# Waiting for the output store at the end of a decode kernel: the wait moves from SyncE to GpSimd

## The chip, the cores and the metric

One core of one Trainium2 chip. The metric is the device time of one execution in microseconds (us). A run can fall into a slower state with a lower granted clock; no run whose state is on record did (granted clocks of 0.766 to 0.771 of full speed), so all of them may be compared. Times inside a trace are counted from the first instruction of the program.

The engines are TensorE (PE in the profile), VectorE (DVE), ScalarE (ACT), GpSimd (POOL) and SyncE (SP). A q behind the name (SPq, POOLq) means the engine's sequencer, which runs its program, waits and issues transfers (DMA). A semaphore is a counter: one side raises it, and another waits until it has reached a value. A barrier is a place that no engine passes before all have reached it.

## The reference

One decoding step: a layer norm of one token, grouped attention over a cache of 65,536 keys and values in eight groups, an output projection, a small feed-forward branch, and the sum.

```python
x = A_x                                   # (1, 1, 512)
xn = _layernorm(x)
# _A_ref: q = xn @ wq, 32 heads on 8 cached K/V heads, softmax over 65536 keys, @ wo
# _B_ref: gelu(xn @ w1 + b1) @ w2 + b2
return x + _A_ref(xn, A_k_cache, A_v_cache, A_wq, A_wo) + _B_ref(xn, B_w1, B_b1, B_w2, B_b2)
```

The K and V caches are 134 MB each in bfloat16 (8 x 65,536 x 128 x 2 bytes). The output is 512 numbers, 1 KB.

## The kernel before

A small recording layer collects every operation with what it reads and writes, and works out the semaphore waits. The engines' programs are then emitted, most of them inside a block. A barrier of the program's own stands at the end of the block; behind it follow the last matmuls, the last cast, the store and the wait for it.

```python
# ... (norm, projections, the loop over K and V, the last matmuls into pR)
sch.op(DVE, lambda: dve.tensor_copy(out=fin_bf[0:NR, :], in_=pR[0:NR, 0:128]),     # L823
       reads=[f"pss{R}"], writes=["fin"])
ev_out = sch.dma(
    SP,
    lambda: sp.dma_start(out=out[0, 0].rearrange("(kt p) -> kt p", p=128),         # L827
                         in_=fin_bf[0:NR:32, :]),
    sem_out, reads=["fin"], writes=["out_dram"],
)
# ...
with nc.Block() as block:                                                          # L842
    # ... each engine's program up to here
    # ...
for e, obj in ((PE, pe), (DVE, dve), (SP, sp)):
    _emit(obj, e.ops[rest[e]:])
sp.wait_ge(ev_out.sem, ev_out.val)                                                 # L866
```

The store's semaphore is number 119; the program waits until it holds 16, which I call full. GpSimd and ScalarE have nothing to do behind the block. GpSimd's last work in the whole kernel is a small memset that passes on the arrival of the last V chunk.

## Time and profile before

| what | before |
|---|---|
| median of the first 3 runs (lowest, highest) | 656.82 us (656.76, 657.03) |
| span of the profiled run, first to last instruction | 655.5 us |
| device time of the same run | 656.81 us |
| read from HBM | 280.50 MB, 428 GB/s |
| last cast / store issued / semaphore full / wait over | 653.79 / 654.46 / 655.46 / 655.49 us |

The page of the kernel before says what bounds it. The DMA row gives the busy share of the DMA engines in 40 slices, in tenths:

```profile
span 655.5 us, 27968 instructions
...
DMA  9999999999999999999999999999999999999997
...
HBM read 280.50 MB, written 0.00 MB: 428 GB/s over the span
## 4 chain that ended last, share of the span: by engine, by line
DMA 63%; PE 34%; issue 2%; DVE 0%; SPq 0%
```

The DMA engines are busy for 90% or more of every slice but the last. Nothing at the end of the kernel can change that; the change can only move the last few microseconds. The chain of waits, in order of time, shows those (start, duration, what; the last pieces, kernel before):

```profile
635.59 17.13 DMA kv<-in_A_wo_dram
652.72 0.14 issue
652.85 0.62 PE pss L805 x16
653.48 0.02 issue
653.50 0.29 DVE fin_bf L823
```

This chain ends with the last instruction that an engine executes, the cast at 653.79 us. It does not hold the store and the wait, which are work of a sequencer. The timeline shows the issue of the store (start, duration, engine, line, what; kernel before):

```profile
653.82 0.64 SPq L827 DMA_DIRECT2D out_dram<-fin_bf  x1
```

And the list of SyncE's own waits shows the wait for it (engine and line, whom it waited for, us in total, times, longest; kernel before):

```profile
SPq L827 <- DVE fin_bf L823: 3.4, 1, 3.4
SPq L866 <- DMA out_dram<-fin_bf: 1.0, 1, 1.0
```

So the span ends with SyncE's wait, at 655.49 us. But the run took 656.81 us, and no view prints what lies in the 1.32 us behind the span. The trace has it all the same: it records every update of every semaphore, those that the program doesn't own too. These are the updates of semaphore 2 near the end, read from these records (us from the span's start; kernel before):

```
first pass :  653.641 653.675 653.714 653.934 | 655.619 655.663 655.701 655.735 655.782
(234 other semaphores, one update each, 655.749 to 656.345)
second pass:  656.569 656.604 656.642 656.685 656.709 656.808 656.846 656.880 656.927
```

I call the updates of a pass moves 1 to 9. The Trainium skill, "Runtime: NRT & Kernel Launch", section "Semaphores 0–2 are reserved", says that semaphore 2 is the runtime's sync barrier. Its section "The ~15µs preamble/postamble breakdown" puts a barrier, a clearing of the semaphores and another barrier behind every kernel, and gives the way through the five engines, for the barrier in front of the kernel, as about 355 ns, 8 hops of 44 ns. This trace agrees in the sum: in the second pass, moves 1 to 9 took 358 ns. The single hops were unequal: 35, 38, 43, 24, 99, 38, 34 and 47 ns. That the single updates between the passes are the clearing is read from their place there and from that section. In nine of the ten profiles of this study the device time is within 0.02 us of move 6 of the second pass (in one, E5, it is 0.135 us later, and why stays open). So I measure the tail from the end of the last wait for the store to that move: 656.808 - 655.493 = 1.315 us before.

### The profile page before, as it was taken

What the parts mean: (1) busy time and instruction counts of PE and PEld (TensorE: products, weight loads), DVE (VectorE), ACT (ScalarE), POOL (GpSimd) and SP (SyncE); (2) the same over time, 40 slices, a digit from 0 to 9 for tenths busy, and PEclk for the clock granted to TensorE, in tenths of its full rate; (3) what the DMA queues carried; (4) which work ended last, traced back from release to release, by engine and by line L of the source; (5) the groups of instructions that cost most, each with busy time, mean ns of one, the idle gap of its engine ahead of it and who ended that gap; (6) DMA issues with size and microseconds to landing.
All of it is one profiled execution on the core that took longest, in us unless ns stands there. A gap on an engine that the chain in (4) does not pass through costs nothing.

```text
span 655.5 us, 27968 instructions
## 1 busy us (share of the span) xinstructions
PE 536.8 (82%) x12682; PEld 509.6 (78%) x12682; DVE 275.8 (42%) x574; ACT 245.0 (37%) x454; POOL 2.9 (0%) x27
## 2 busy tenths in 40 slices
PE   2478699989789697878969788896978879797897
PEld 0277598979788696878959687895978879697886
DVE  3244072625436171453516245261534516154353
ACT  0134162634425162352506235160443516145251
POOL 0000000000000000000000000000000000000000
PEclk9788596967869596786959679595886959578695
DMA  9999999999999999999999999999999999999997
GB/s 386 445 431 422 431 430 432 446 422 450 416 448 420 428 460 404 436 428 454 430 420 440 426 442 422 426 460 408 444 426 450 430 418 436 428 460 404 432 432 305
DMA packets 8774, 280.65 MB, mean 428 GB/s; under 512 B 1082, under 2 KB 1596, under 8 KB 1724
## 3 DMA queue, kind: packets, MB, share of 16 engines
q1 hardware_dynamic: 8616, 280.50, 99.4%
q8 instruction: 8, 0.13, 0.1%
q10 hardware_dynamic: 148, 0.01, 0.0%
q14 instruction: 2, 0.02, 0.0%
HBM read 280.50 MB, written 0.00 MB: 428 GB/s over the span
## 4 chain that ended last, share of the span: by engine, by line
DMA 63%; PE 34%; issue 2%; DVE 0%; SPq 0%
DMA kv<-in_A_k_cache_dram 61%; PE pst L590 27%; PE pss L610 4%; DMA kv<-in_A_wo_dram 3%; PE pO L681 2%; PE pA L637 0%; PE pA L648 0%; DVE pmax L618 0%; PE pA L697 0%; PE pss L805 0%; DVE gmax L639 0%; DVE diag L641 0%; SPq L470 0%; SPq L467 0%; DVE fin_bf L823 0%
## 5 line engine op out<-in xcount | busy, mean ns | idle before, releaser
L600 ACT ACTIVATE kt_ring<-pst 128x1024 bf16<-128x1024 bf16 x192 | 195.6, 1027 | 310.6 <-PE pst L590 309.2
L590 PE MATMUL pst<-ident_bf,kv 128*128 128x128 bf16 x4096 | 281.8, 235 | 34.5 <-DMA kv<-in_A_k_cache_dram 34.4
L590 PEld LDWEIGHTS pst<-ident_bf,kv 128*128 128x128 bf16 x4096 | 263.5, 107 | 42.8 <-DMA kv<-in_A_k_cache_dram 35.9
L598 DVE COPY kt_ring<-pst 128x1024 bf16<-128x1024 bf16 x320 | 210.7, 687 | 119.1 <-PE pst L590 116.9
L681 PE MATMUL pO<-P_bf,kv 128*128 128x4 bf16 x4096 | 115.1, 166 | 37.6 <-DMA kv<-in_A_v_cache_dram 31.2
L681 PEld LDWEIGHTS pO<-P_bf,kv 128*128 128x128 bf16 x4096 | 113.6, 104 | 38.9 <-DMA kv<-in_A_v_cache_dram 32.2
L610 PE MATMUL pss<-q_cur,kt_ring 128*128 128x4 bf16 x4096 | 111.9, 164 | 5.1 <-issue 5.1
L610 PEld LDWEIGHTS pss<-q_cur,kt_ring 128*128 128x128 bf16 x4096 | 109.3, 96 | 5.3 <-issue 5.3
L659 ACT ACTIVATE P_bf<-pss,negm 128x128 bf16<-128x128 f32 x128 | 50.9, 548 | 67.4 <-DVE negm L651 67.4
L690 DVE COPY o_all<-pO 128x4 f32 (+1 forms) x32 | 5.2, 162 | 120.7 <-PE pO L681 119.9
L618 DVE TENSOR_REDUCE pmax<-pss 128x4 f32<-128x512 f32 x32 | 22.1, 692 | 69.0 <-PE pss L610 69.0
L659 ACT ACTIVATION_READ_ACCUMULATOR P_bf<-pss,negm 128x1 f32 x128 | 35.4, 277 | 0.0
L648 PEld LDWEIGHTS pA<-diag,ones_f 4*128 4x128 f32 x64 | 12.6, 244 | 18.1 <-DVE diag L641 16.5
L637 PE MATMUL pA<-ident_f,pmax 128*4 128x128 f32 x64 | 14.2, 310 | 12.6 <-DVE pmax L618 12.6
L648 PE MATMUL pA<-diag,ones_f 4*128 4x4 f32 x64 | 15.4, 309 | 10.0 <-DVE diag L641 10.0
L637 PEld LDWEIGHTS pA<-ident_f,pmax 128*4 128x4 f32 x64 | 2.9, 84 | 15.7 <-DVE pmax L618 14.0
L639 DVE TENSOR_REDUCE gmax<-pA 4x1 f32<-4x128 f32 x32 | 8.8, 274 | 9.4 <-PE pA L637 9.4
L673 DVE COPY sums_all<-sums 128x8 f32 (+1 forms) x16 | 2.7, 172 | 23.4 <-ACT P_bf L659 23.4
L697 PE MATMUL pA<-sums_all,ones_f 128*128 128x128 f32 x32 | 12.4, 491 | 0.0
L518 PE MATMUL pA<-ones_bf,xn_row 1*128 1x1 bf16 x4 | 0.3, 172 | 12.7 <-DVE xn_row L514 12.7
L518 PEld LDWEIGHTS pA<-ones_bf,xn_row 1*128 1x128 bf16 x4 | 0.2, 115 | 12.7 <-DVE xn_row L514 12.7
L651 DVE TENSOR_SCALAR negm<-pA 128x4 f32<-128x4 f32 x32 | 5.1, 161 | 10.8 <-PE pA L648 10.8
(78 smaller groups left out, 63.8 us busy)
## 6 DMA issues: line engine op xcount, KB each, us to landing
kv<-in_A_k_cache_dram SPq DMA_DIRECT2D x32, 4096.0 KB, 27.5
kv<-in_A_v_cache_dram SPq DMA_DIRECT2D x4, 4096.0 KB, 23.1
kv<-in_A_wq_dram SPq DMA_DIRECT2D x1, 4096.0 KB, 12.3
kv<-in_B_w_dram SPq DMA_DIRECT2D x2, 1792.0 KB, 17.8
kv<-in_A_wo_dram SPq DMA_DIRECT2D x1, 2048.0 KB, 23.7
kv<-in_A_wo_dram SPq DMA_DIRECT2D x1, 1024.0 KB, 25.9
kv<-in_A_wo_dram SPq DMA_DIRECT2D x1, 512.0 KB, 26.6
kv<-in_A_wo_dram SPq DMA_DIRECT2D x1, 384.0 KB, 17.1
```

Source lines behind the costliest of these rows:

```text
L590: lambda tb=tb, at=at, b=b, tt=s * TPB + t: pe.transpose(pst[tb][:, at * 128:(at + 1) * 128], slot[b][:, tt, :], ident_bf[:, :]),
L598: e, fn = DVE, lambda tb=tb, dst=dst: dve.tensor_copy(out=dst, in_=pst[tb][:, :])
L600: e, fn = ACT, lambda tb=tb, dst=dst: act.activation(out=dst, in_=pst[tb][:, :], func=ACTF.Copy)
L610: lambda k=k, kb=kb, at=at, t=t: pe.matmul(pss[k][:, at:at + HPG], lhsT=kt_ring[:, kb * BCOL + t * 128:kb * BCOL + (t + 1) * 128], rhs=q_c ...
L618: lambda k=k: dve.tensor_reduce(out=pmax[:, :], in_=pss[k][:, 0:CW].rearrange("p (t j) -> p j t", j=HPG), axis=AX.X, op=ALU.max),
L637: sch.op(PE, lambda: pe.matmul(pA[0:HPG, PA_ST:PA_ST + 128], lhsT=pmax[:, 0:HPG], rhs=ident_f[:, :], start=True, stop=True), reads=["pmax" ...
L639: sch.op(DVE, lambda: dve.tensor_reduce(out=gmax4[:, :], in_=pA[0:HPG, PA_ST:PA_ST + 128], axis=AX.X, op=ALU.max), reads=["pA"], writes=[" ...
L648: sch.op(PE, lambda: pe.matmul(pA[:, PA_SB:PA_SB + HPG], lhsT=ones_f[0:HPG, 0:128], rhs=diag4[0:HPG, 0:HPG], start=True, stop=True), reads ...
L659: lambda k=k, at=at, j=j, src=src: act.activation(out=P_v[k][:, :, j], in_=src[:, :, j], func=ACTF.Exp, bias=negm[:, at:at + 1], scale=1.0 ...
L681: lambda k=k, t=t: pe.matmul(pO[:, 0:HPG], lhsT=vslot[:, k * TPD + t, :], rhs=P_v[k][:, t, :], start=t == 0, stop=t == TPD - 1),
L690: sch.op(DVE, lambda: dve.tensor_copy(out=o_all[:, at_pair(i, PW, k * HPG, HPG)], in_=pO[:, 0:HPG]), reads=["pO"], writes=[f"o{k}"])
L697: sch.op(PE, lambda: pe.matmul(pA[:, PA_SUM:PA_SUM + NC], lhsT=ones_f[:, :], rhs=sums_all[:, :], start=True, stop=True), reads=["ones_f", ...
```

## The change

```diff
     for e, obj in ((PE, pe), (DVE, dve), (SP, sp)):
         _emit(obj, e.ops[rest[e]:])
-    sp.wait_ge(ev_out.sem, ev_out.val)
+    pool.wait_ge(ev_out.sem, ev_out.val)
```

The intent: some engine must wait until the output has landed, and SyncE has just issued the store. If GpSimd, which has been idle, waits, SyncE can end its program about 1 us earlier. No other instruction moves on any engine.

## The prediction

> **What bounds the kernel.** The stream of the K and V caches from HBM. The page shows the DMA engines at nine tenths or more in every slice but the last, 280.5 MB at 428 GB/s over a span of 655.5 us; the chain that ended last is 63% DMA. The change touches none of it: the instruction order of all engines is the same in both programs, except that the wait for the store's semaphore ends GpSimd's program instead of SyncE's. Only the last microseconds can move.
>
> **The tail before** (from the span's start; timeline, SyncE's own waits, and the trace's records of semaphore updates, which no view prints). The last cast ends at 653.79. SyncE issues the store from 653.82 to 654.46. Its semaphore is full at 655.46; SyncE's wait ends at 655.49, the span's end (SyncE's waits: 1.0 us for the output's DMA). The profiled run took 656.81 us, so 1.32 us lie behind the span. There the records show semaphore 2 move nine times: 653.64, 653.68, 653.71, 653.93, a gap, then 655.62, 655.66, 655.70, 655.74, 655.78. Then all semaphores are cleared until 656.35, and semaphore 2 moves nine times again from 656.57; the sixth move is at 656.81, the device time. The Trainium skill, "Runtime: NRT & Kernel Launch" (sections on reserved semaphores and on the preamble/postamble breakdown), says that semaphore 2 is the runtime's sync barrier, a serpentine through five engines at about 44 ns a hop. This trace agrees: undisturbed hops are 34 to 47 ns.
>
> The order, read from who was late: move 1 follows PE's last matmul, moves 2 and 3 follow at once (ScalarE and GpSimd, long idle), move 4 comes 0.14 us after VectorE's cast, move 5 0.13 us after SyncE's wait. So SyncE is the chain's far end, and the late engine sat in the best place: all others had checked in, and four hops back (0.16 us) released everybody.
>
> **What the change does.** The store's issue, its landing (1.0 us) and one engine's wake stay. Nothing leaves the critical path; SyncE's early end only buys idle time in the barrier. Added: GpSimd, third (or second) in the chain, arrives last, so the hops through VectorE (44 ns) and SyncE (24 ns) come after the store. VectorE must also post its up-move and get ready for the way back: where it had not waited long (second barrier), move 6 came 0.12 us after move 4, against 0.04 us after move 5 in the first. Estimate from these records: move 3 at 655.62, 4 at 655.66, 5 at 655.69, 6 at 655.79, 9 at 655.91 instead of 655.78: +0.12 us (+0.16 if GpSimd is second). Clearing and second barrier follow unchanged.
>
> **Prediction.** 656.95 us, 0.1 us slower in the mean, hidden in the 0.27 us by which three runs of before differ. 8 in 10: 656.2 to 657.7. Faster by over 2%: 0.005; within 2%: 0.99; slower: 0.005.
>
> **What would show it.** The span stays 655.5 us, ended by GpSimd's semaphore wait; SyncE's waits lose the 1.0 us entry. In the semaphore records, moves 1 and 2 of semaphore 2 come before the store lands, moves 3 to 9 in one run after it, with 0.12 us from move 4 to 6. From the wait's end to the second barrier's sixth move: 1.44 us instead of 1.32.
>
> **What would make it wrong.** GpSimd needing much longer or shorter than SyncE (0.13 us) from its wait to its barrier move; SyncE having slow closing work of its own behind the wait, then hidden, turning the sign to a gain of some tenths; jitter of the HBM stream, larger than the effect.

## The result

| | before | after |
|---|---|---|
| device time, median of 4 runs (lowest, highest) | 656.88 us (656.76, 657.03) | 657.27 us (657.13, 657.44) |
| span of the profiled run | 655.5 us | 655.5 us |
| its device time | 656.81 us | 657.34 us |
| tail: end of the wait to move 6 of the second pass | 1.315 us | 1.864 us |

The ratio is 1.0006 (95% interval 0.9989 to 1.0023). A ratio is the mean time of one kernel's fast runs over that of the other's of the same rounds, so not quite the ratio of the medians. The four runs of each kernel don't overlap, though (of the 18 later runs of before, the slowest took 657.13 us), and the tail tells why: it grew by 0.55 us. I put the difference between 0.39 us and 0.55 us down to the span, which moves by some tenths from run to run (655.3 to 655.6 us in the four runs of after).

Page of the kernel after:

```profile
span 655.5 us, 27968 instructions
...
DMA  9999999999999999999999999999999999999997
...
DMA 64%; PE 34%; issue 2%; DVE 0%; SPq 0%
```

The last pieces of its chain of waits in order of time:

```profile
635.90 16.78 DMA kv<-in_A_wo_dram
652.68 0.14 issue
652.82 0.62 PE pss L805 x12
653.44 0.02 issue
653.47 0.29 DVE fin_bf L823
```

The issue of the store in its timeline:

```profile
653.78 0.64 SPq L827 DMA_DIRECT2D out_dram<-fin_bf  x1
```

The end of its list of SyncE's waits:

```profile
SPq L827 <- DVE fin_bf L823: 3.1, 1, 3.1
SPq L880 <- PEq L880: 0.2, 1, 0.2
```

SyncE's entry for L866 is gone. The instruction of that line, looked up in the kernel after, is now GpSimd's (duration in ns, then start in us):

```profile
L866 POOLq EVENT_SEMAPHORE  x1: 17/17/17, 655.5 to 655.5; - x1
```

Inside the span, then, nothing happened: stream, cast, issue (0.64 us) and landing are the same, and a waiting GpSimd wakes about as fast as a waiting SyncE (41 ns from the full semaphore to the wait's end, against 34 ns). Behind the span, the semaphore records differ. Here are both passes again, kernel after; GpSimd's wait ended at 655.467 us:

```
first pass :  653.608 653.642 | 656.005 656.049 656.072 656.177 656.215 656.251 656.298
(247 other semaphores, one update each, 656.195 to 656.869)
second pass:  657.093 657.127 657.165 657.209 657.232 657.331 657.370 657.404 657.450
```

Moves 1 and 2 come before the store lands, moves 3 to 9 after it, as predicted for a GpSimd that stands third. But move 3 comes 0.538 us after the end of GpSimd's wait, where SyncE's move 5 had come 0.126 us after the end of SyncE's. That term had been taken as equal. I call it the closing time of an engine.

### The profile page after: what moved, and what is told of

The parts are those of the page before. It is cut to its first block, busy times and chain, and to the rows that moved or that the text cites. A ratio compares the mean times of both kernels' runs of the same rounds, so it can differ in the third digit from the quotient of the medians.

```text
span 655.5 us, 27968 instructions
## 1 busy us (share of the span) xinstructions
PE 537.6 (82%) x12682; PEld 509.7 (78%) x12682; DVE 275.6 (42%) x574; ACT 245.2 (37%) x454; POOL 2.9 (0%) x27
## 4 chain that ended last, share of the span: by engine, by line
DMA 64%; PE 34%; issue 2%; DVE 0%; SPq 0%
DMA kv<-in_A_k_cache_dram 61%; PE pst L590 27%; PE pss L610 4%; DMA kv<-in_A_wo_dram 3%; PE pO L681 2%; PE pA L637 0%; PE pA L648 0%; DVE pmax L618 0%; PE pA L697 0%; PE pss L805 0%; DVE gmax L639 0%; DVE diag L641 0%; SPq L470 0%; SPq L467 0%; DVE fin_bf L823 0%
```

## The experiments

The theory (A): an engine has a fixed closing time between its last instruction and its move in the runtime's barrier; GpSimd's is four times SyncE's; to it come the hops that the barrier still has to make after a late engine. The rivals: (B) any engine other than SyncE, or any that waits for a store that it didn't issue, is slow; (C) SyncE has closing work of its own that its early end now hides; (D) the slowness comes of waiting for a DMA; (E) it is a stall of GpSimd's sequencer at that wait, or depends on where the instruction stands in its program.

All eight kernels gave correct results. "Time minus span" is the mean over all timed runs of a kernel, not over the profiled one alone; the spans are listed to 0.1 us. Closing time and tail are from the semaphore records of the profile. A closing time in brackets was waited out by nobody.

| run | who waits | median us | time minus span | closing us | tail us |
|---|---|---|---|---|---|
| before (18 runs beside E1 to E8) | SyncE | 656.79 and 656.82 | 1.37 and 1.34 | 0.126 | 1.315 |
| after | GpSimd | 657.27 | 1.85 | 0.538 | 1.864 |
| E1 | ScalarE | 656.94 | 1.56 | 0.125 | 1.483 |
| E2 | VectorE | 656.89 | 1.45 | 0.162 | 1.451 |
| E3 | TensorE | 657.15 | 1.65 | 0.200 | 1.590 |
| E4 | GpSimd and SyncE | 657.39 | 1.91 | 0.538 | 1.859 |
| E5 | SyncE; GpSimd waits for the cast | 656.69 | 1.34 | (0.537) | 1.318 |
| E6 | GpSimd, four waits in a row | 657.45 | 1.90 | 0.538 | 1.954 |
| E7 | GpSimd, three more waits before | 657.34 | 1.88 | 0.538 | 1.858 |
| E8 | SyncE; ScalarE issues | 656.75 | 1.36 | 0.117 | 1.309 |

The two medians of before are those of the nine runs beside E1 to E4 and of the nine beside E5 to E8; the two groups ran on different chips. None of the ratios leaves the verdict "same" (0.9998 to 1.0009, and every interval holds 1), so the reasons rest on the records, where single hops of some tens of ns can be seen. Each closing time and tail is from one profile; the mean "time minus span" of all runs, within 0.08 us of the tail for every kernel, is what supports them.

### E1: ScalarE waits

```diff
-    sp.wait_ge(ev_out.sem, ev_out.val)
+    act.wait_ge(ev_out.sem, ev_out.val)
```

> ScalarE waits for the store, SyncE issues it and ends. W is the end of the wait. Theory A (the slow 0.54 us from the wait's end to the barrier move is GpSimd's own; any engine early in the chain costs only the hops after it): ScalarE moves semaphore 2 (move 2 of 9) at W+0.13 us, moves 3 to 5 follow in 0.11 us, move 6 comes 0.13 us after move 4; from W to the second barrier's sixth move 1.48 us (before 1.32, after 1.86); time 657.0 us. Rival B (0.5 us is what any engine pays that waits for a store which it did not issue, or that is not last in the chain): move 2 at W+0.5 us, tail 1.85 to 1.9 us, time 657.3 to 657.4.

The wait ended at 655.625 us, and the first pass was:

```
653.761 | 655.750 655.788 655.832 655.856 655.961 655.999 656.035 656.082
```

Move 2 came 0.125 us after the wait, and the tail was 1.483 us. That is theory A's 1.48. Rival B falls: ScalarE neither issued the store nor stands at the end of the chain, and it closes as fast as SyncE. Long idleness is no cause of the slow close either: ScalarE's last work ended at 642.19 us, 13.4 us before its wait did, and GpSimd's in the kernel after at 643.22 us, 12.2 us before.

### E2: VectorE waits

```diff
-    sp.wait_ge(ev_out.sem, ev_out.val)
+    dve.wait_ge(ev_out.sem, ev_out.val)
```

> VectorE waits for the store. Theory A: moves 1 to 3 come before the store lands, move 4 at W+0.13 us, move 5 0.02 us later, move 6 0.13 us after move 4; tail from W 1.40 us, time 656.9 to 657.0 us. Rival B: move 4 at W+0.5 us, tail 1.8 us, time 657.3.

The wait ended at 655.126 us. Moves 1 to 3 came before the store landed, move 4 at 655.288, move 5 at 655.311 and move 6 at 655.414 us. So VectorE stands fourth. Its closing time is 0.162 us, a little more than expected, and the tail 1.451 us instead of 1.40.

### E3: TensorE waits

```diff
-    sp.wait_ge(ev_out.sem, ev_out.val)
+    pe.wait_ge(ev_out.sem, ev_out.val)
```

> TensorE waits for the store. It is first in the chain, so no engine can check in before it. Theory A: no move of semaphore 2 before the store lands; move 1 at W+0.15 us, moves 2 to 5 in the next 0.14 us, move 6 0.13 us after move 4; tail from W about 1.55 us, time 657.1 us. Rival B: move 1 at W+0.5 us, tail 1.9 us or more, time 657.4 or more.

The wait ended at 655.222 us, and all nine moves came after it:

```
| 655.422 655.457 655.495 655.538 655.562 655.667 655.705 655.741 655.787
```

So TensorE stands first. Its closing time is 0.200 us (0.15 expected), the tail 1.590 us (1.55 expected). With E1, E2 and the two kernels of the change, the order is now shown for every engine by who holds up which move: TensorE, ScalarE, GpSimd, VectorE, SyncE, then back.

### E4: both wait

```diff
+    pool.wait_ge(ev_out.sem, ev_out.val)
     sp.wait_ge(ev_out.sem, ev_out.val)
```

> Both GpSimd and SyncE wait for the store. Theory A (SyncE's early end buys nothing; GpSimd alone sets the tail): SyncE is ready 0.13 us after W while GpSimd moves at W+0.54 us, so moves 3 to 9 and the tail are as in the changed kernel: 1.86 us, time 657.3 us. Rival C (SyncE ending early hides some closing work of SyncE): the tail grows by that work, to 1.95 us or more.

SyncE has its wait back, as the list of its waits shows (run E4):

```profile
SPq L827 <- DVE fin_bf L823: 2.9, 1, 2.9
SPq L867 <- DMA out_dram<-fin_bf: 1.0, 1, 1.0
```

Yet GpSimd's wait ended at 655.552 us, move 3 came at 656.090, 0.538 us later, and the tail was 1.859 us, as in the kernel after. The early end of SyncE is worth nothing beside a waiting GpSimd, because SyncE is ready before GpSimd's move arrives. This run alone could not see closing work of SyncE that hides within GpSimd's 0.54 us; what bounds that work is the trace of before, where all of it took 0.126 us. The two together settle rival C.

### E5: GpSimd waits for the cast, SyncE for the store

```diff
+    pool.wait_ge(DVE.sem, DVE.count)
     sp.wait_ge(ev_out.sem, ev_out.val)
```

> GpSimd waits for the last cast (done about 1.7 us before the store lands), SyncE keeps the wait for the store. Theory A (GpSimd needs a fixed 0.54 us from its last wait to its barrier move, whatever it waited for): move 3 about 0.54 us after the end of GpSimd's wait, near 654.35 us, move 4 right after it, both before the store lands, so nothing of it is paid: moves 5 to 9 and the tail of 1.32 us as before, time 656.8 us. Rival D (the 0.54 us comes of waiting for the store's DMA): move 3 at 0.13 us after the wait, near 653.95 us.

GpSimd's wait for VectorE's cast ended at 653.732 us. The first pass:

```
653.529 653.563 | 654.269 654.313 | 655.512 655.555 655.594 655.628 655.675
```

Move 3 came 0.537 us after a wait that has nothing to do with a DMA. Rival D falls. And the tail was 1.318 us, because the slow closing was over before the store landed at 655.353 us. The cost is thus not that GpSimd closes slowly, but that it closes slowly as the last engine. The median is 0.13 us below that of before, but with the same tail, so I put it down to the stream's jitter and count no gain.

### E6 and E7: three more waits, after or before

```diff
-    sp.wait_ge(ev_out.sem, ev_out.val)
+    pool.wait_ge(ev_out.sem, ev_out.val)
+    for _ in range(3):                          # E6
+        pool.wait_ge(ev_out.sem, ev_out.val)
```

> GpSimd waits for the store four times in a row (the last three are already met). If the 0.54 us is fixed work behind the last instruction, it follows the last of the four unchanged, and the three more add what three sequencer steps cost [...]: tail from the first wait's end 1.87 + 0.2 = 2.05 to 2.1 us, time 657.5. Rival E (the 0.54 us is a stall that starts at the first wait, for example a fetch of what follows it): the three waits vanish in it, or the 0.54 us behind the last one shrinks or grows clearly; tail near 1.87.

```diff
-    sp.wait_ge(ev_out.sem, ev_out.val)
+    for _ in range(3):                          # E7
+        pool.wait_ge(POOL.sem, POOL.count)
+    pool.wait_ge(ev_out.sem, ev_out.val)
```

> Control for the run with more waits after: the same number of instructions in GpSimd's program, but the three added waits stand before the wait for the store and are met long before. Fixed work: wait to move 3 stays 0.54 us, tail 1.86 us, time 657.3. If the place of the last instruction in the program mattered (rival E): another value than 0.54.

The build merged the waits in pairs, so each program has one instruction more than the kernel after, not three; in E7 the store's wait shares its instruction with one of the added waits. An instruction with two waits took 42 or 43 ns instead of 17. In E6 the two ended at 655.494 and 655.585 us, and move 3 came at 656.123, 0.538 us after the second. In E7 the wait ended at 655.311 us and move 3 came at 655.849, again 0.538 us later. Rival E falls, as far as one more instruction can tell: what is added in front of the closing is paid in addition, and the closing itself doesn't change.

E6's total of 2.045 us from its first wait's end fits the expected 2.05 to 2.1, but partly by luck. The added instruction cost 0.091 us, less than the 0.2 us expected for three. Another 0.09 us came between the two passes (656.414 to 657.300, 0.886 us, against 0.795 us in the kernel after). It is in one profile, and its cause stays open.

### E8: ScalarE issues, SyncE waits

```diff
     ev_out = sch.dma(
-        SP,
-        lambda: sp.dma_start(out=out[0, 0]...
+        ACT,
+        lambda: act.dma_start(out=out[0, 0]...
 ...
-for e, obj in ((PE, pe), (DVE, dve), (SP, sp)):
+for e, obj in ((PE, pe), (DVE, dve), (SP, sp), (ACT, act)):
```

(ScalarE's last operation is also kept out of its block, as SyncE's is.)

> ScalarE issues the store, SyncE does nothing but wait for it. Whether the barrier's cost depends on who waits, not on who issues: wait's end to move 5 stays 0.13 us and the tail 1.32 us, as before. The time changes only by how long ScalarE takes to issue (its three small loads took 0.21 to 0.52 us against SyncE's 0.64 us for this store): between -0.3 and +0.1 us, 656.5 to 656.9 us. If the issuer's closing matters, move 2 comes late and the tail is over 1.4 us.

The timeline of E8 shows ScalarE's issue:

```profile
653.11 0.29 DVE L823 CAST fin_bf<-pss 97x128 bf16<-97x128 f32 x1 [5.09 <-PE pss L805]
653.44 0.61 ACTq L827 DMA_DIRECT2D out_dram<-fin_bf  x1
```

The issue took 0.61 us instead of 0.64. From its start to the full semaphore were 1.661 us (653.438 to 655.099), against 1.640 us before (653.819 to 655.459). Nothing is gained there, and the tail is 1.309 us as before. The difference of the medians, 0.07 us, is the span's. One thing was not expected in this form: move 2, ScalarE's, came at 654.661 us, 0.61 us after the recorded end of its issue, where after a plain wait (E1) it had come after 0.125 us. That cost nothing, because the store landed later still. So ScalarE, when it issues the store, checks in late, and that hides behind the landing. ScalarE's closing time is thus not one fixed number: theory A's "fixed" holds here for a program that ends with a wait. For SyncE as the issuer no run shows it.

No run beats the kernel before by more than its jitter, and the records say why none of the five places could: SyncE and ScalarE close fastest (0.12 to 0.13 us), and SyncE has the fewest hops left after it.

## Why the prediction was right or wrong

- 657.27 us lies in 656.2 to 657.7, and the time stayed within 2%. The sign was right as well. But that the range held is in part luck: it is 1.5 us wide, so it held although the tail grew over four times as much as predicted.
- "Nothing leaves the critical path; SyncE's early end only buys idle time in the barrier" held. E4 shows it: giving SyncE its wait back left the tail at 1.859 us.
- The span stayed at 655.5 us and is ended by GpSimd's semaphore wait; SyncE's entry of 1.0 us is gone. Both as predicted.
- "Moves 1 and 2 before the store lands, moves 3 to 9 in one run after it, with 0.12 us from move 4 to 6" held. The last interval measured 0.128 us.
- What failed is one term of the sum: the prediction put move 3 at 655.62, which is GpSimd's closing time taken to be SyncE's 0.13 us. It was named as a risk ("GpSimd needing much longer or shorter than SyncE"), not priced. It measured 0.538 us, in the kernel after and in E4, E6 and E7 alike, and 0.537 us in E5.

The sum, with what was measured in the two profiles:

| term | predicted us | measured us |
|---|---|---|
| closing time of the last engine, GpSimd's less SyncE's | 0 | 0.538 - 0.126 = +0.412 |
| from its move to move 6 (3 to 6 after, 5 to 6 before) | +0.12 | 0.172 - 0.044 = +0.128 |
| move 6 of the first pass to move 6 of the second | 0 | 1.154 - 1.145 = +0.009 |
| growth of the tail | +0.12 | +0.549 |

So the tail was predicted at 1.44 us and measured 1.864. What GpSimd does in its 0.54 us is not shown: the trace holds no instruction of the runtime's part of the program. That it was the same in five profiles of this kernel, on at least two chips, with the wait moved by 1.7 us, one instruction added, and another semaphore waited for, is shown. What it consists of, and whether it is the same in another kernel or behind other work than a wait, stays open.

## What to carry to other kernels

The program's last instruction is not the end of the measured time: behind it every engine closes and goes through the runtime's barrier in a fixed order, and the semaphore records of the trace show that tail where the printed views stop. In this kernel's runs that makes a rule to try and to measure again: let the final wait stand on the engine whose closing time is short and which is last in that order, here SyncE, and let GpSimd end early, where its slow closing hides. An idle engine is not a free engine to wait on: ending SyncE 1 us earlier was worth nothing, since the last engine to check in decides.

## What the Trainium skill lacked or had wrong

- "Runtime: NRT & Kernel Launch", section "The ~15µs preamble/postamble breakdown": it gives the barrier's hops but not the order of the engines, nor that a late engine costs more the earlier it stands. The runs show TensorE, ScalarE, GpSimd, VectorE, SyncE, with tails of 1.590, 1.483, 1.864, 1.451 and 1.315 us for the same wait. Without each engine's closing time these are 1.390, 1.358, 1.326, 1.289 and 1.189 us.
- No place that I read has an engine's closing time between the end of its last wait and its barrier move: 0.125 us for ScalarE, 0.117 to 0.126 for SyncE, 0.162 for VectorE, 0.200 for TensorE and 0.538 for GpSimd.
- "Runtime: NRT & Kernel Launch", section "The ~15µs preamble/postamble breakdown", also gives the clearing of the semaphores behind the kernel as about 1.5 us. Here the updates read as the clearing took 0.60 us (655.749 to 656.345), and 0.60 to 0.67 us in the ten profiles; the time from the wait's end to the second barrier's sixth move was 1.315 us in all.
- "Perfetto Trace Analysis", section "DMA Instruction — HWDGE (DVE, Sync)", says that at the recorded end of such an instruction the sequencer has made its semaphore increments and is free. Here the first update of the store's semaphore came 0.37 us after the recorded end (654.456 to 654.828), still before the store's first recorded packet (655.049), and ScalarE's barrier move in E8 came 0.61 us after the recorded end of its issue, against 0.125 us after a plain wait. That raises a doubt and refutes nothing: who made the first update, how long it was on its way, and when the sequencer was really free are not shown.
